# One order for all pieces of an mLSTM and MLP kernel, with output stores on another queue and merged loads

## The chip, the cores and the metric

The kernel runs on one core of a Trainium2 chip. The metric is the device time of one execution in microseconds (us); less is better. The engines named below are PE (matrix products), PEld (its weight loads), DVE (vector), ACT (scalar and activation), POOL, and SP, which here does nothing but issue transfers and wait. Each takes its instructions in program order.

## The reference

A gated linear recurrence (mLSTM) feeds a two-layer MLP. Batch 4, 8 heads, 768 tokens, head size 40; the MLP has 320 inputs, 2048 hidden columns and 320 outputs on 3072 tokens.

```
m_new = max(f[t] + m, i[t]);  fs = exp(f[t] + m - m_new);  is = exp(i[t] - m_new)
C = fs * C + is * outer(v[t], k[t]);   n = fs * n + is * k[t]
y[t] = sigmoid(o[t]) * (C @ q[t]) / max(|n . q[t]|, 1)
h = y @ w_in;   g = h * sigmoid(h);   out = g @ w_out
```

## The kernel before, in words

The recurrence is computed in chunks of 128 tokens. A **unit** n is one chunk of one batch row, all eight heads; there are 24, and chunk c of a row needs the state that chunk c-1 left. `perform` (L871) reads the string `ORDER` (L50 to L102) word by word and emits each word's instructions; the place of a word in the string is its place in the stream of every engine that it uses. The words of a unit, in the order in which one unit needs them:

- `qk`, `kvo`, `d`, `lq` (L445 to L480): loads on SP's queue of q and k (two transfers of 160 KB), of k, v and the output gate, of the decay matrix D (four transfers) and of the decays (four).
- `s` (L493): for units 0 to 3, PE spreads the decays into PSUM instead of `d`; `e` (L513): eight exponentials on ACT; `k` (L522): POOL's causal mask; `r`, `l`, `t`: small ACT pieces; `v` (L538): DVE weights v; `q` (L553): POOL scales q.
- `S` (L615) scores and `P` (L560) products on PE, `w` (L618) and `c` (L576) on DVE, `c` with a POOL multiply between two DVE operations.
- `V` (L622) and `Q` (L640): values and state queries on PE. `V` ends with a `nop` on SP that waits for V's last matmul, and Q's first matmul waits for that nop (the fence, L637). Where a unit's scores go half by half into one bank, L612 puts another such nop on SP. A transfer that stands behind a nop on SP is issued after it.
- `g` (L660) gates and normalizes on DVE in five operations, `x` (L680) transposes on PE, `h` and `y` (L692, L696) split the result into a rounded high part and a rest.

The weights arrive as 64-bit floats and are turned into 32-bit values on the chip, in eight parts each of w_in (`i0` to `i7`, with `c0` and `c4` for its last 64 rows) and w_out (`o0` to `o7`). The words of a part are `L` load (SP), `M` (ACT), `S`, `Z`, `J` (DVE, L318 to L347), and for w_in `T` (ACT, L364) and `R` (DVE, L369). `gs gu gm go gt gf` are the gate scans of one chunk, mostly DVE, `gf` with small matmuls; `go` stores the decays to DRAM.

The MLP of units 0 to 3 is the **opening** (512 tokens): per hidden block of 128 columns `m` (PE, L712), `a` (ACT, L750), `b` (DVE, L755), `n` (PE, L766 to L769), as kinds A (units 0 and 1), B (2 and 3) and J (all four, blocks 4 to 15). The other units come two by two in **steps** 1 to 10. A step has eight slots (`slot`, L906); a slot is 16 matmuls of the first product (L712), tanh and multiply (`glu`, L813), a split into high and low (`halves`, L822) and 12 matmuls of the second product (L841) of two slots earlier. `place` (L930) hangs the pieces of the units onto the slots: at slots 2 and 5 of a step stand P, V, S and Q. When a step's last second product is done, `put` (L721) copies each unit's result on ACT and issues its store on ACT's own queue (L725). `split_out` (L382) rounds w_out in the first eight slots of step 1. `z*8` (`spin`, L862) is eight bf16 matmuls on constants at the start.

In `ORDER`, the blocks of the opening's MLP from block 4 on come in pairs: load and convert the next parts, two `m`, two `n`, one unit's attention. The lines below are four such lines.

```
Lo3 Mi2 Si2 Zi2 Ji2 Ti2 Ri2
Mo2 So2 Zo2 Jo2
mJ4 aJ4 bJ4
mJ5 aJ5 bJ5
```

Of the kernel before, what the change touches and what calls it, by code (L numbers as in the profile page):

```python
# [50 lines left out]
qk0 kvo0 gs0 gu0 gm0 go0 gt0 z*8 s0.0 s0.1 gf0 lq0 Li0 Lc0 qk1 kvo1 Lo0 Mi0 e0.0 e0.1 r0 k0.0 k0.1 v0 S0.0 S0.1 P0 l0 q0 w0 c0  # L51
Si0 Zi0 Ji0 Ti0 Ri0 Mc0 Sc0 Zc0 Jc0 Tc0 Rc0 s1.0 s1.1 lq1 e1.0 e1.1 r1 k1.0 k1.1 v1 P1 V0 S1.0 S1.1 Q0 t0 g0 x0 h0 y0 l1 q1 w1 c1 Li1 qk2 qk3 Mo0 So0 Zo0 Jo0
kvo2 s2.0 s2.1 lq2 e2.0 e2.1 r2 k2.0 k2.1 v2 P2 V1 S2.0 S2.1 Q1 t1 g1 x1 h1 y1 l2 q2 w2 c2 mA0 aA0 bA0 mA1 aA1 bA1 Mi1 Si1 Zi1 Ji1 Ti1 Ri1 Lo1 Li2
nA0 nA1 mA2 aA2 bA2 kvo3 s3.0 s3.1 lq3 e3.0 e3.1 r3 k3.0 k3.1 v3 P3 V2 S3.0 S3.1 Q2 t2 g2 l3 q3 w3 c3 x2 h2 y2 Mo1 So1 Zo1 Jo1 V3 mA3 aA3 bA3 Q3 t3 g3 x3 h3 y3 nA2 nA3 gs1 gu1 gm1 gt1 gf1 go1 gs2 gu2 gm2 gt2 gf2 go2
mB0 aB0 bB0 mB1 aB1 bB1 nB0 nB1 mB2 aB2 bB2 mB3 aB3 bB3 nB2 nB3
Li3
Lo2 Mi2 Si2 Zi2 Ji2 Ti2 Ri2
Mo2 So2 Zo2 Jo2
mJ4 aJ4 bJ4
mJ5 aJ5 bJ5  # L60
qk4 kvo4 d4 lq4 k4.0 k4.1 e4.0 e4.1 v4 l4
Li4 Lc4
Lo3 Mi3 Si3 Zi3 Ji3 Ti3 Ri3
Mo3 So3 Zo3 Jo3
mJ6 aJ6 bJ6
nJ4
mJ7 aJ7 bJ7
nJ5
S4.0 P4 S4.1 w4 q4 c4
Li5  # L70
Lo4 Mi4 Si4 Zi4 Ji4 Ti4 Ri4
Mc4 Sc4 Zc4 Jc4 Tc4 Rc4
Mo4 So4 Zo4 Jo4
mJ8 aJ8 bJ8
nJ6
mJ9 aJ9 bJ9
nJ7
qk5 kvo5 d5 lq5 k5.0 k5.1 e5.0 e5.1 v5 l5
Li6
Lo5 Mi5 Si5 Zi5 Ji5 Ti5 Ri5  # L80
Mo5 So5 Zo5 Jo5
# [24 lines left out]
def mlstm_mlp_kernel(  # L106
# [614 lines left out]
    def put(n, halves, ob):  # L721
        c, b = n // B, n % B
        for cs, po in halves:
            nc.scalar.activation(ob[:, cs], po, AF.Copy, scale=0.5)
        nc.scalar.dma_start(out[b * S + c * L : b * S + (c + 1) * L, :], ob)  # L725

    class Opening:
# [31 lines left out]
        def mm2(self, kind, fc):  # L759
# [3 lines left out]
            for u in sorted(range(u0, u1), key=lambda u: -(u > 2)):  # L763
# [8 lines left out]
                if last and u == 2:  # L772
                    self.store(2)
                if last and u == 1:
                    for k in (0, 1, 3):
                        self.store(k)

        def store(self, u):
# [10 lines left out]
            if u >= 2:
                big.give(f"ob{u}")  # L790

    class Step:
# [19 lines left out]

        def glu(self, s):  # L813
            j, ph = self.j, self.ph.pop(s)
            th = p2.tile([128, FPS * NT], F32, tag="th", name=f"th{j}_{s}")
# [4 lines left out]
            self.g[s] = th  # L820

        def halves(self, s):  # L822
            j, g = self.j, self.g[s]
            t = p3.tile([128, 2, FPS * NT], F32R, tag="g", name=f"g{j}_{s}")
            gh, gl = t[:, 0], t[:, 1]
            nc.scalar.copy(gh, g)  # L826
            nc.vector.tensor_tensor(out=gl, in0=g, in1=gh.bitcast(F32), op=ALU.subtract)  # L827
            self.g[s] = (gh, gl)
# [41 lines left out]

    def perform(order):  # L871

        for word in order.split():
# [1 line left out]
            what, n, hf, times = m[1], m[2] and int(m[2]), m[3] and int(m[3]), int(m[4] or 1)
            u = units[n] if what in UNIT else None
            for _ in range(times):
                if what in UNIT:
                    f = getattr(u, UNIT[what])
                    f() if hf == "" or hf is None else f(hf)  # L880
                elif what in PART:
                    getattr(part[what[-1] + str(n)], PART[what])()
                elif what in GATE:
                    getattr(first, GATE[what])(n, 1)
                elif what in MLP:
# [171 lines left out]
```

## Time and profile before

| what | us |
|---|---|
| median of three runs (lowest to highest) | 578.83 (577.93 to 580.23) |
| the profiled execution: its own time | 580.62 |
| its span, first to last instruction | 578.9 |
| start of the opening's first product (mA0) | 50.68 |
| start of step 1's first product | 197.78 |
| start of step 3's first product | 282.16 |

The profile lists every instruction with its start, its length and what released it. A line such as "PE psum<-xh,wh x8 [4.37 <-ACT wh L364]" reads: eight matmuls, before the first of which PE was idle for 4.37 us until ACT's instruction at L364 was done. PEclk is the share of the full TensorE clock that was granted; 1.0 is 2.4 GHz, 0.5 is 1.2 GHz. Before 54.1 us the trace holds no record of the clock and shows 1.00.

### The profile page before, as it was taken

The numbers are of one execution on the slowest core, as the hardware profiler recorded it, in microseconds if no ns is written. First come the engines' busy times: TensorE is split into PE (matmuls) and PEld (weight loads), VectorE is DVE, ScalarE is ACT, GpSimd is POOL, SyncE is SP. The second block draws the span as 40 slices with busy tenths as digits, with TensorE's granted clock in tenths as the row PEclk, the third lists the DMA queues.
The fourth block names the chain that finished last, engine by engine and source line by source line (L and its number), as shares of the span: only waits on it lengthen the run. The fifth ranks groups of instructions, "written<-read, shape, count | busy, mean of one in ns | idle before, by whom it ended". The sixth has DMA issues, their size and how long they took to land.

```text
span 578.9 us, 13625 instructions
## 1 busy us (share of the span) xinstructions
PE 484.7 (84%) x5760; PEld 444.2 (77%) x5760; DVE 274.6 (47%) x541; ACT 220.0 (38%) x512; POOL 88.4 (15%) x127
## 2 busy tenths in 40 slices
PE   5256678566866888998998989989899899899997
PEld 3245557344744777998998989989899899899997
DVE  1543264545355266655455544554554445444332
ACT  2322212423123065544454335434444345433332
POOL 2321201102011012201222022210221222100000
PEclk9999678687867898999999989999999899999999
DMA  5343008143060352332133221320223203000000
GB/s 164 102 129 128 2 6 245 40 139 112 9 205 2 89 164 68 89 98 77 26 112 87 71 70 59 112 89 26 88 87 108 80 12 110 2 25 1 1 24 23
DMA packets 26269, 44.63 MB, mean 77 GB/s; under 512 B 4384, under 2 KB 16608, under 8 KB 26208
## 3 DMA queue, kind: packets, MB, share of 16 engines
q1 hardware_dynamic: 22688, 39.75, 23.3%
q10 hardware_dynamic: 3520, 4.01, 2.0%
q8 instruction: 45, 0.74, 0.5%
q14 instruction: 16, 0.13, 0.1%
HBM read 39.71 MB, written 4.03 MB: 76 GB/s over the span
## 4 chain that ended last, share of the span: by engine, by line
PE 60%; issue 16%; DVE 11%; ACT 6%; DMA 3%; POOL 2%; SPq 1%; ACTq 0%; DVEq 0%; POOLq 0%
PE psum L712 31%; PE psum L841 16%; DVE th L817 3%; ACT th L816 3%; PE psum L568 2%; DMA D<-LFd 2%; PE psum L601 2%; PE psum L766 2%; DVE D L620 2%; PE psum L649 2%; PE psum L630 2%; PE psum L684 1%; DVE vw L542 1%; ACT D L518 1%; POOL qt L555 1%
## 5 line engine op out<-in xcount | busy, mean ns | idle before, releaser
L841 PE MATMUL psum<-woh,g 128*128 128x320 f32 x640 | 153.9, 310 | 0.0
L712 PE MATMUL psum<-xh,wh 128*128 128x256 f32 x480 | 140.6, 300 | 5.3 <-DVE D L620 4.7
L712 PE MATMUL psum<-xl,wh 128*128 128x256 f32 x480 | 135.2, 289 | 0.0
L841 PEld LDWEIGHTS psum<-woh,g 128*128 128x128 f32 x640 | 110.8, 189 | 0.0
L712 PEld LDWEIGHTS psum<-xh,wh 128*128 128x128 f32 x480 | 94.3, 197 | 11.0 <-DVE D L620 9.2
L816 ACT ACTIVATE th<-psum 128x512 f32<-128x512 f32 x80 | 47.8, 597 | 137.7 <-PE psum L712 125.4
L841 PE MATMUL psum<-wol,g 128*128 128x320 f32 x320 | 99.0, 309 | 0.0
L817 DVE SCALAR_TENSOR_TENSOR th<-th,psum 128x512 f32<-128x512 f32 x80 | 54.9, 686 | 84.7 <-ACT th L816 84.7
L712 PEld LDWEIGHTS psum<-xl,wh 128*128 128x128 f32 x480 | 94.5, 197 | 0.4 <-DVE xl L698 0.3
L712 PE MATMUL psum<-xh,wl 128*128 128x256 f32 x320 | 92.4, 289 | 0.0
L827 DVE TENSOR_TENSOR g<-th,g 128x512 fp32r<-128x512 f32 x80 | 59.0, 738 | 54.9 <-ACT g L826 53.6
L712 PE MATMUL psum<-X,wh 128*128 128x512 f32 (+1 forms) x120 | 44.2, 467 | 32.4 <-ACT wh L364 29.6
L826 ACT CAST g<-th 128x512 fp32r<-128x512 f32 x80 | 49.5, 619 | 53.4 <-DVE th L817 48.4
L712 PEld LDWEIGHTS psum<-xh,wl 128*128 128x128 f32 x320 | 63.1, 197 | 0.0
L841 PEld LDWEIGHTS psum<-wol,g 128*128 128x128 f32 x320 | 60.5, 189 | 0.0
L712 PEld LDWEIGHTS psum<-X,wh 128*128 128x128 f32 x120 | 27.5, 258 | 40.4 <-ACT wh L364 32.6
L524 POOL TENSOR_SCALAR_AFFINE_SELECT D<-D 64x512 f32<-64x512 f32 x48 | 34.8, 724 | 114.3 <-DMA D<-LFd 81.3
L586 POOL TENSOR_TENSOR S<-S,eq 104x164 f32<-104x164 f32 x20 | 9.3, 464 | 246.9 <-DVE S L584 242.8
L568 PE MATMUL psum<-vw,kvo 64*64 64x41 f32 x704 | 17.9, 244 | 33.0 <-DVE vw L542 33.0
L568 PEld LDWEIGHTS psum<-vw,kvo 64*64 64x64 f32 x704 | 14.9, 149 | 38.7 <-DVE vw L542 35.9
L518 ACT ACTIVATE D<-D,aT 128x64 f32<-128x64 f32 x160 | 41.7, 334 | 5.3 <-POOL D L524 5.3
L555 POOL TENSOR_TENSOR qt<-raw,eq 104x512 f32<-104x512 f32 x24 | 30.8, 1285 | 39.4 <-issue 39.2
(114 smaller groups left out, 558.8 us busy)
## 6 DMA issues: line engine op xcount, KB each, us to landing
kvo<-in_kvo_dram SPq DMA_DIRECT2D x24, 484.0 KB
raw<-in_qk_dram SPq DMA_DIRECT2D x48, 160.0 KB
wro<-in_w_out_dram SPq DMA_DIRECT2D x8, 640.0 KB
D<-LFd SPq DMA_DIRECT2D x80, 64.0 KB
wri<-in_w_in_dram SPq DMA_DIRECT2D x8, 512.0 KB
lq<-LFd SPq DMA_DIRECT2D x96, 40.0 KB
out_dram<-ob ACTq DMA_DIRECT2D x24, 160.0 KB
wrc<-in_w_in_dram SPq DMA_DIRECT2D x4, 256.0 KB
```

The lines of the kernel that those rows point to most:

```text
L518: nc.scalar.activation(d[:, j, :], e[:, j, :], AF.Exp, bias=aT[:, self.c, hf, r : r + 1])
L524: nc.gpsimd.affine_select(out=d, in_=d, compare_op=ALU.is_ge, fill=0.0 if self.n < WIDE else NEG, base=0, pattern=[[0, H], [1, LB]], chann ...
L555: nc.gpsimd.tensor_tensor(out=self.qt, in0=self.q[:KP], in1=self.eq, op=ALU.mult)
L568: nc.tensor.matmul(Z[hf * 64 : (hf + 1) * 64, k * HF + j, D1 : 2 * D1], self.kt[rs, h * D : h * D + 64], self.vw[rs, h, :], start=True, st ...
L601: m = nc.tensor.matmul(self.ps[r * 64 : (r + 1) * 64, hf, j, :], self.k[rows, r ^ hf, j, :], self.q[rows, r ^ hf, j, :], start=True, stop= ...
L620: nc.vector.tensor_tensor(out=d, in0=self.ps, in1=d, op=ALU.mult)
L712: nc.tensor.matmul(ph, w, x, start=(i == 0), stop=(i == len(ops) - 1))
L816: nc.scalar.activation(th, ph, AF.Tanh, scale=0.5)
L817: nc.vector.scalar_tensor_tensor(out=th, in0=th, scalar=1.0, in1=ph, op0=ALU.add, op1=ALU.mult)
L826: nc.scalar.copy(gh, g)
L827: nc.vector.tensor_tensor(out=gl, in0=g, in1=gh.bitcast(F32), op=ALU.subtract)
L841: nc.tensor.matmul(self.po[t], g[:, ts], w, start=(fc == 0 and i == 0), stop=(last and i == len(ops) - 1),)
```

## The change

`ORDER` now holds the whole program, the steps included; `slot`, `place` and what calls them are gone, and `tanh`, `glu`, `high` and `low` are words of their own (`a`, `b`, `f`, `F`), as are the two halves of `split_out` (`uh`, `ul`), the copy of a result (`O`) and its store (`D`). `m1.0` is the first product of slot 0 of step 1. From `m3.0` on the words stand in the sequence in which `slot` and `place` emitted them. Up to there the sequence is new. Its words up to `m1.0`:

```
Li1 gs0 Mi1 gu0 gs1 Lc0 gm0 kvo0 Si1 gt0 z7*23 s0.1 gu1 gf0 Zi1 go0 Mc0 s0.0 Sc0 s1.0 qk0 gm1 s1.1 e0.0 Zc0 gt1 Jc0 e0.1
r0 Tc0 Li0 v0 k0.1 Ji1 Rc0 lq0 kvo1 z7*11 S0 k0.0 e1.1 Mi0 l0 lq1 w0 e1.0 P0 Si0 qk1 r1 c0 kvo2 Zi0 s2.1 lq2 t0 qk2 v1
q0 Ti1 e2.1 Ji0 s2.0 z7*12 V0 k1.1 l1 Q0 g0 Lo0 s3.1 e2.0 r2 k1.0 z7*1 S1 Ti0 w1 P1 t2 q1 e3.1 s3.0 c1 t1 e3.0 kvo3 v2
gf1 z7*3 V1 qk3 Ri0 Lo1 r3 go1 Q1 P2 l2 Ri1 k2.1 g1 k2.0 z2*1 x0 S2 c2 lq3 w2 h0 x1 Mo0 z7*3 V2 Li2 Lo2 q2 Q2 S3 h1 y1
So0 y0 k3.0 g2 k3.1 t3 v3 Zo0 mA0 mA2 aA0 bA0 l3 P3 mA1 w3 lq4 c3 x2 Mo1 Li4 So1 V3 aA2 qk4 bA2 Jo0 aA1 q3 mA3 d4 h2 Zo1
Mi2 y2 Li3 d5 nA0 aA3 Jo1 Q3 Mo2 g3 Mi4 nA2 x3 bA3 Si2 Lc4 bA1 h3 l4 Zi2 y3 nA3 Ji2 Ti2 So2 k4.1 nA1 mB0 Li5 kvo4 Ri2
Zo2 mJ4 aB0 aJ4 kvo5 bB0 mB2 nB0 aB2 gs2 bJ4 k5.1 Si4 Mc4 bB2 Jo2 Mi3 Zi4 Lo3 Si3 Ji4 k5.0 Sc4 k4.0 mJ5 Zc4 e4.1 e4.0
aJ5 Ti4 nB2 v4 mB1 Zi3 Li6 bJ5 q4 Jc4 aB1 bB1 Ji3 e5.0 nJ4 nJ5 S4.0 Lo4 Ti3 lq5 P4 Tc4 Ri4 qk5 Lo5 Ri3 t5 S4.1 Mi6 Li7
c4 gu2 mJ6 aJ6 Rc4 e5.1 nB1 mJ7 Mo3 bJ6 Mo4 gm2 w4 mJ9 V4 v5 S5.0 So3 Zo3 Si6 So4 Q4 qk6 gt2 Jo3 t4 Mi5 Lo7 l5 aJ7 go2
Lo6 S5.1 Si5 aJ9 P5 Zi5 bJ7 bJ9 nJ6 d6 lq6 g4 mJ8 Zo4 mB3 Ji5 k6.0 Jo4 w5 Zi6 k6.1 aB3 Ji6 d7 aJ8 bJ8 Mo5 nJ7 Ti5 Ri5
So5 x4 lq7 h4 nJ9 Zo5 Mo7 bB3 mJ10 Ti6 Jo5 aJ10 c5 y4 mJ11 kvo6 q5 lq8 gf2 e6.0 bJ10 Ri6 gl Mi7 V5 S6.0 Si7 So7 Q5 e6.1
k7.0 aJ11 Zi7 Ji7 S6.1 v6 mJ12 w6 kvo8 gs3 nJ10 nB3 qk7 Mo6 g5 Ti7 Zo7 nJ8 Ri7 k7.1 l6 d8 bJ11 So6 x5 mJ15 aJ12 h5 t6
bJ12 Zo6 nJ11 kvo7 mJ13 P6 q6 l8 Jo6 V6 aJ15 bJ15 d9 e7.0 aJ13 k8.0 mJ14 c6 l7 nJ12 k8.1 uh0 uh1 bJ13 aJ14 Q6 qk8 y5
bJ14 m1.0
```

`z7*23` is 23 spins into PSUM bank 7. The rest of the change:

```diff
@@ load_raw: q and k
-                    t[hf * 64 : hf * 64 + D].rearrange("p w k j t -> p (w k j t)"), qk[n, hf]
+                    t[hf * 64 : hf * 64 + D].rearrange("p w k j t -> p w (k j t)"),
+                    qk[n, hf].rearrange("p (w f) -> p w f", w=2),
@@ load_d: two transfers in place of four (load_lq: the same)
+            hs, ks = NC * 2 * NB * LB, NB * LB
             for r in range(2):
-                for hf in range(2):
...
+                at = LFd[0, c, r, b * HF : (b + 1) * HF]
+                nc.sync.dma_start(
+                    self.Dm[r * 64 : (r + 1) * 64].rearrange("p (f j) t -> p f (j t)", f=2),
+                    bass.AP(at.tensor, at.offset, [[0, 64], [hs + (1 - 2 * r) * ks, 2], [1, HF * LB]]),
+                )
@@ products: P's first matmul waits for the last Q before it
+                        if first and Unit.fenced:
+                            after(m, Unit.fenced)
+                        first = False
@@ queries
+            Unit.fenced = nc.sync.nop()
+            after(Unit.fenced, m)
@@ put becomes copy (ACT) and sent (SP)
-        for cs, po in halves:
-            nc.scalar.activation(ob[:, cs], po, AF.Copy, scale=0.5)
-        nc.scalar.dma_start(out[b * S + c * L : b * S + (c + 1) * L, :], ob)
+        nc.sync.dma_start(out[b * S + c * L : b * S + (c + 1) * L, :], obs.pop(n))
```

## Rows read from the trace of the kernel before

**Rows 1.** The page: the span, and busy time by engine.
```profile
span 578.9 us, 13625 instructions
PE 484.7 (84%) x5760; PEld 444.2 (77%) x5760; DVE 274.6 (47%) x541; ACT 220.0 (38%) x512; POOL 88.4 (15%) x127
PE   5256678566866888998998989989899899899997
```

**Rows 2.** Busy time by stretch: opening, steps 1 and 2, step 3, the rest.
```profile
core 0: us, PE busy (x) PEld busy (x) DVE busy (x) ACT busy (x) POOL busy (x), PEclk, DMA share, GB/s
0.00:197.80 197.80, 126.54 (x1253) 98.18 (x1253) 86.55 (x169) 52.34 (x130) 28.78 (x45) 0.83 0.33 97
197.80:282.10 84.30, 77.71 (x986) 73.35 (x987) 48.26 (x98) 42.21 (x102) 18.30 (x26) 0.94 0.34 97
282.10:319.20 37.10, 35.05 (x488) 33.95 (x487) 18.82 (x38) 16.97 (x41) 7.25 (x10) 1.00 0.26 78
282.10:578.90 296.80, 280.42 (x3524) 272.67 (x3522) 139.82 (x275) 125.41 (x281) 41.37 (x56) 0.99 0.19 58
```

**Rows 3.** Waits, 0 to 198 us: total us, times, longest; SP's own last.
```profile
PE psum L712 <- ACT wh L364: 29.6, 7, 7.0
PE psum L568 <- DVE vw L542: 21.3, 4, 8.6
PE psum L684 <- DVE x L674: 8.2, 5, 1.7
...
SPq L612 <- PE psum L601: 70.9, 3, 24.4
SPq L637 <- PE psum L630: 49.6, 6, 19.0
```

**Rows 4.** Timeline of one opening pair, 122.2 to 126.9 us: start, length, instruction.
```profile
122.23 0.37 SPq L297 DMA_DIRECT2D wri<-in_w_in_dram  x1
...
124.27 0.42 DVE L320 TENSOR_SCALAR wti<-wti 128x512 uint32<-128x512 uint32 x1
...
126.18 0.62 ACT L364 CAST wh<-wti 128x512 fp32r<-128x512 f32 x1 [6.15 <-DVE wti L340]
...
126.85 1.22 PE L712 MATMUL psum<-X,wh 128*128 128x512 f32 x2 [4.37 <-ACT wh L364]
```

**Rows 5.** Busy time in a stretch at 0.5 and one at 1.0 of the clock.
```profile
125.80:136.00 10.20, 8.20 (x19) 5.67 (x19) 7.19 (x11) 3.83 (x6) 1.94 (x2) 0.50 0.87 253
115.60:125.70 10.10, 6.88 (x87) 5.24 (x86) 3.21 (x7) 1.16 (x2) 0.46 (x1) 1.00 0.22 69
```

**Rows 6.** DVE's timeline: its first scan, and a hand-over to POOL and back.
```profile
3.32 0.42 DVE L197 TENSOR_TENSOR_SCAN G<-G 48x128 f32<-48x128 f32 x1 [2.38 <-DMA G<-in_ig_dram]
...
49.85 0.68 DVE L620 TENSOR_TENSOR D<-psum,D 128x512 f32<-128x512 f32 x1
...
51.74 0.32 DVE L587 TENSOR_TENSOR S<-S,psum 104x164 f32<-104x164 f32 x1 [0.98 <-POOL S L586]
```

**Rows 7.** PE's timeline: one matmul of 512 columns at either clock, and the eight spins.
```profile
1.00 3.60 PE L864 MATMUL psum<-G 128*128 128x512 bf16 x8 [1.00 <-DVE G L898]
...
117.28 0.40 PE L712 MATMUL psum<-X,wl 128*128 128x512 f32 x1
...
127.87 0.63 PE L712 MATMUL psum<-X,wl 128*128 128x512 f32 x1
```

**Rows 8.** Timeline of step 3's end: result copies, their stores, and the next attention.
```profile
402.07 0.44 ACT L724 ACTIVATE ob<-psum 128x320 f32<-128x320 f32 x1 [0.66 <-PE psum L841]
...
402.90 0.66 PE L630 MATMUL psum<-kvo,D 64*64 64x41 f32 x32
402.93 0.44 ACT L724 ACTIVATE ob<-psum 128x320 f32<-128x320 f32 x1 [0.41 <-ACT ob L724]
...
403.39 0.34 ACTq L725 DMA_DIRECT2D out_dram<-ob  x1
```

**Rows 9.** The page: packets of SP's queue and its share of the 16 DMA engines.
```profile
q1 hardware_dynamic: 22688, 39.75, 23.3%
```

More of the change, by code (lines that the diff above doesn't have):

```diff
@@ L50 @@
 ORDER = """
[L51 to L81, printed above, removed]
@@ L391, in split_out, with split_low @@
             wol[i] = wraw.take("wol0", [128, 2, DM], F32R)
-        nc.scalar.copy(hi, full)
-        nc.vector.tensor_tensor(out=wol[i], in0=full, in1=hi.bitcast(F32), op=ALU.subtract)
+        nc.scalar.copy(rounded(slice(2 * i, 2 * i + 2)), wo[i])
+    def split_low(i):
+        hi = rounded(slice(2 * i, 2 * i + 2))
+        nc.vector.tensor_tensor(
+            out=wol[i], in0=wo.pop(i), in1=hi.bitcast(F32), op=ALU.subtract
+        )
     parts = []
@@ L430, in mlstm_mlp_kernel @@
     class Unit:
+        fenced = None
         def __init__(self, n):
@@ L562, in products @@
             self.pu = [Z[:KP, k * HF : (k + 1) * HF, D1 : 2 * D1] for k in range(2)]
+            first = True
             for j in range(HF):
@@ L771, in mm2, with copy @@
                     )
[L772 to L778, printed above, removed]
+        def copy(self, u):
             if u < 2:
@@ L819, in glu, with high, low @@
             )
[L820 to L828, printed above, removed]
+        def high(self, s):
+            t = p3.tile([128, 2, FPS * NT], F32R, tag="g", name=f"g{self.j}_{s}")
+            self.g[s] = t[:, 0], t[:, 1]
+            nc.scalar.copy(t[:, 0], self.th[s])
+        def low(self, s):
+            gh, gl = self.g[s]
+            nc.vector.tensor_tensor(
+                out=gl, in0=self.th.pop(s), in1=gh.bitcast(F32), op=ALU.subtract
+            )
         def mm2(self, s):
@@ L869, in mlstm_mlp_kernel, with gate_word @@
     opening = steps[0] = Opening()
+    late = []
+    def gate_word(what, n):
+        if what == "gl":
+            late.append(gates_late())
+        elif n < 3:
+            getattr(first, GATE[what])(n, 1)
+        else:
+            getattr(late[0], GATE[what])(3, NC - 3)
+            if what == "gf":
+                big.give("lfi", "lml")
     def perform(order):
@@ L874, in perform @@
             m = re.fullmatch(r"([a-zA-Z]+)(\d*)(?:\.(\d))?(?:\*(\d+))?", word)
[L875 to L885, printed above, removed]
-                    getattr(opening, MLP[what])(what[-1], n)
-                else:
-                    spin(1)
+            what, n, k, times = m[1], int(m[2] or 0), m[3] and int(m[3]), int(m[4] or 1)
+            if what in UNIT:
+                getattr(units[n], UNIT[what])(*([] if k is None else [k]))
+            elif what in STEP:
+                getattr(steps[n], STEP[what])(k)
+            elif what in PART:
+                getattr(part[what[-1] + str(n)], PART[what])()
+            elif what in OTHER:
+                OTHER[what](n)
+            elif what in MLP:
+                getattr(opening, MLP[what])(what[-1], n)
+            elif what == "z":
+                spin(times, n)
+            else:
+                gate_word(what, n)
+    STEP = dict(m="mm1", a="tanh", b="glu", f="high", F="low", n="mm2")
     UNIT = dict(qk="load_raw", kvo="load_kvo", d="load_d", lq="load_lq", s="spread", e="exps",
@@ L897, in mlstm_mlp_kernel @@
     MLP = {a + b: f for a, f in dict(m="mm1", a="tanh", b="glu", n="mm2").items() for b in "ABJ"}
+    OTHER = dict(uh=split_high, ul=split_low, O=copied, D=sent)
     nc.vector.memset(busy, 1.0)
     perform(ORDER)
-    def run(*calls):
-        for f in calls:
-            f()
-    def slot(j, s, first=(), early=(), middle=(), end=()):
-        st = steps[j]
-        run(*first)
-        st.mm1(s)
-        run(*early)
-        st.glu(s)
-        run(*middle)
-        if s >= LAG:
-            st.mm2(s - LAG)
-        elif j > 1:
-            steps[j - 1].mm2(NSL - LAG + s)
-        else:
-            opening.mm2("J", NFC - LAG + s)
-        st.halves(s)
-        run(*end)
@@ L962, in mlstm_mlp_kernel @@
-    for n in range(DONE, NU):
-        place(n)
-    late = gates_late()
-    rest = (3, NC - 3)
-    at(0, "end", lambda: late.scan(*rest))
-    at(1, "middle", lambda: late.sub(*rest))
-    at(2, "middle", lambda: late.sum(*rest))
-    at(2, "end", lambda: late.store(*rest))
-    at(3, "middle", lambda: late.top(*rest))
-    at(4, "first", lambda: late.flip(*rest), lambda: big.give("lfi", "lml"))
-    for i in range(DFF // 256):
-        at(i, "middle", lambda i=i: split_out(i))
-    for j in range(1, NSTEP):
-        for s in range(NSL):
-            slot(j, s, **pieces.get((j - 1) * NSL + s, {}))
@@ L978, in mlstm_mlp_kernel @@
-    for s in range(NSL - LAG, NSL):
-        steps[NSTEP - 1].mm2(s)
 def _layout(inputs):
```

155 lines of the change are left out of this document (71 added, 84 removed).

## The prediction

> **What bounds the kernel now.** I read the page first [rows 1]: PE is busy for 484.7 of 578.9 us, far more than DVE or ACT, so PE is the engine to follow, and 94 us of the span are without it. The question is where these lie. The sums by stretch [rows 2] answer it: step 3 takes 37.10 us with PE busy for 35.05, and from the start of step 3 to the end it is 280.42 of 296.80. There only 16 us are to be had, and the change leaves the sequence of those words as it was. The opening is another matter: 197.80 us, with PE busy for 126.54, DVE for 86.55, ACT for 52.34, and DMA at a share of 0.33. No engine is full. Steps 1 and 2 are nearly full (77.71 of 84.30).
>
> The waits of the opening [rows 3] say what PE stood for: 29.6 us in seven waits for a rounded weight part (`T`, L364), 21.3 us in four for `v`, 8.2 us for `g`'s result. SP, which issues all loads, stood for 120.5 us in its two kinds of nop. One pair shows how these hang together [rows 4]: SP issues the next weight part only after a score fence, DVE begins the three conversions of the part before it at 124.27, ACT rounds at 126.18 after 6.15 us of idling, and PE starts 4.37 us late. Load, convert, multiply and attend stand one after another in the string, and each engine takes them in that order. So the opening is bounded by hand-overs, not by work.
>
> The clock follows from this. In a stretch in which PE was busy for 8.20 of 10.20 us after such a wait the granted share was 0.50, the lower level of 1.2 GHz; in another, busy for 6.88 of 10.10 after dense products, it was 1.00, the 2.4 GHz level [rows 5]. A 512-column matmul takes 0.63 us at the one and 0.40 at the other, the pipeline's tail included [rows 7].
>
> **The parts and their costs.** (a) The opening up to `m1.0`. The words are the same; the new string only puts them side by side, so the time cannot fall below the fullest engine's work. For DVE that is the 86.55 us of before [rows 2] plus what now precedes `m1.0`: `w6` 0.68, `c6` 0.65 (two of 0.32) [rows 6] and the scan `gs3` (384 columns, by the 128-column scan's 0.42 about 1.1 with its copy), together 89 us. For PE it is 126.54 plus 46 more spins, which cost 0.45 us each at the lower clock (eight in 3.60 [rows 7]) and by the ratio of the two levels half of it at the upper, so 10 to 21 us, plus the moved `V6` and `Q6` of 0.66 us each [rows 8]. That is 138 to 149 us if the clock stays as it was. If it is mostly up, the products shrink towards 0.40 for 0.63: 126.54 x 0.63 is 80, and with spins and attention 92 us. So DVE and PE come out nearly equal, and what they wait for each other decides.
>
> DVE's waits in the new sequence, in order. It starts at 3.32 us, when the gates land [rows 6]. It then works some 3.5 us and stops at `gf0`, whose matmuls stand behind 23 spins: these end between 8 and 11 us (all low after the first eight, or all high), so about 3 us. Seven `c`, each with a POOL multiply between two DVE operations that stand next to each other, wait 0.98 us each [rows 6]: 7 us. About ten places remain where a part waits for ACT or for a raw buffer that a `J` has just freed (`Jo3` then `Mi5` then `Si5` is one), at about 1 us: 10 us. I add 7 us for `b` and `g` behind PE where the clock is down. Sum 30, so `m1.0` starts at 89 + 30 = 119 us. The bounds are 104 (half of the waits) and 150 (the clock as before, next part). The gain is 197.8 - 119 = 79 us.
>
> (b) `m1.0` to `m3.0`. PE's words are the same but for `nJ13` more and `V6`, `Q6` fewer, which cancel at some 1.3 us. PE was busy for 77.71 us at a mean clock of 0.94 [rows 2]; 10 us at half clock cost it 5 of these, so 72.7 at the upper level. With step 3's idling (2.05 in 37.10) it comes to 77 us, bounds 73 and 84.3: a gain of 7.
>
> (c) From `m3.0` on: 296.8 as before [rows 2]. Two things are new there. The stores move from ACT to SP: ACT no longer loses the 0.41 us behind each [rows 8], but its waits end on DVE and PE there, so I count nothing. On SP the two stores of a step stand ahead of the next unit's V fence. ACT finishes the second copy at 403.37 in the old sequence and about 0.4 us earlier without its own store; SP then issues a store (0.34), by 403.4, and V ends at 403.56 [rows 8]. It just fits. If it does not, Q comes up to 0.4 us late in each of eight steps, 3 us: bounds 0 and 3. The nop behind every Q delays the q and k loads that follow on SP by Q's length, under 1 us; they are for three units later. In the opening P waits for that nop: P2 stands directly behind Q1, whose nop is behind three issues on SP, so some 1.5 us, which is among the ten places of (a).
>
> (d) Loads. Merging four D and four decay transfers into two each halves their issues on SP, which is hidden, since SP waited for 120 us anyway [rows 3]. About 20 MB land before `m1.0` (97 GB/s for 197.8 us [rows 2]); at the 253 GB/s that a share of 0.87 gave [rows 5] the engines would carry 290, so 69 us of 119: hidden, though no longer far off. The 2 KB packets add 80 a unit. SP's queue took 23.3% of 16 engines for 22688 packets [rows 9], 95 ns each; nine units bring 720 more, 4.3 us of all engines if each costs a full one, nothing if bytes alone count. I take nothing, since half of the engines' time is free. The Trainium skill's page "DMA: Bandwidth & Descriptors", section "Rules for kernel authors", speaks against this part: many small transfers should be made into one large one; by it the 4.3 us would be paid, and the forecast would be 497. No run here shows packets of either size side by side.
>
> Sum: 119 + 77 + 296.8 = 492.8 us of span, against 578.9. Around the span lie 580.62 - 578.9 = 1.7 us, so 494.5 for the profiled execution; that one stood 1.8 us above the median of 578.83. Predicted: **493 us**.
>
> **The rivals.** *The clock stays down.* Up to `mA0` the new string mixes short attention matmuls with waits, and the clock may fall there and after each wait, as it did before [rows 5]. PE then needs its 138 to 149 us, and is the bound: `m1.0` at 150, and with 80 for (b) the result is 150 + 80 + 296.8 - 0.1 = 527. For it: 0.50 was granted even at 80% busy. Against: most stops that PE made before, 59 us [rows 3], are what the new sequence fills, and spins stand ahead of `S0`, `V0`, `V1` and `V2`. The Trainium skill's page "TensorE: Matmul & The Clock Gate", section "Loop structure matters more than you think", states that bursts of matmuls between long waits run cold; rows 4 and 5 agree (a 4.37 us wait, then 0.50).
>
> *The hand-overs nearly vanish.* DVE runs with half of my waits, `m1.0` at 104, (b) at 73: 104 + 73 + 296.8 - 0.1 = 474. For it: ACT works only 52 us, and there are always two or three units and two parts in flight. Against: three raw buffers for units, three for parts, two PSUM banks for the products.
>
> *The old serial order half returns.* With buffers as few as before, loads behind the 17 nops before `m1.0` come late at a few places, and half of the 79 us comes back: 532. *Slower than before.* The same nops on SP decide: the longest waits were 24.4 and 19.0 us [rows 3]. If four times a weight part that DVE needs next is queued behind a V or Q that itself waits that long, 4 x 22 = 88 us come on top of 493, and the kernel is at 581; from there every further one makes it slower. From `o0` on the load of a part stands 22 to 87 words ahead of its `M`, which speaks against it. *No effect:* the waits were not what bounds the opening, and it stays near 579.
>
> **How the numbers follow.** My forecast (478 to 508) has 0.5, the quick case 0.15, the clock 0.2, the half return 0.1, slower 0.03 and no effect 0.02. The range takes in the quick case and the clock's and reaches into the half return: 468 to 530; above and below stay about 0.2. A measurement of this kernel tells about 0.5% from no change. Faster by more than that: 0.95; within: 0.02; slower: 0.03.
>
> **What the new profile would show.** Right: PE's L712 with X starts before 42 us; `m1.0`, the first L712 with xh, near 119; DVE busy for about 75% up to it; SP's waits at L637 no longer followed by a PE wait for L364; 297 us from the start of step 3. Wrong: a granted clock of 0.50 over half of 40 to 119 us (the clock); PE waiting for `T` or `v` by more than 20 us in the opening (the serial order); DMA share over 0.8 for tens of us; a remainder over 300 us (the stores on SP).

## The result: 494.1 us, and the profile after

Median 494.11 us of four runs (490.88 to 495.18), against 579.48 (577.93 to 580.23) for four runs of the kernel before beside it: ratio 0.852, 95% interval 0.848 to 0.857. The profiled execution took 493.72 us. The first products of each stage in the two profiled executions:

| first product of | before, us | after, us | gained up to there |
|---|---|---|---|
| block 0 of the opening (mA0) | 50.68 | 44.25 | 6.4 |
| block 4, the first J (mJ4) | 99.00 | 60.34 | 38.7 |
| step 1 (m1.0) | 197.78 | 121.94 | 75.8 |
| step 3 (m3.0) | 282.16 | 196.78 | 85.4 |
| end of the span | 578.9 | 492.0 | 86.9 |

(At mJ4 the two have not done the same work: after, three of the four B blocks and the gate scan of chunk 2 still lie behind it.) The page after, against [rows 1]; PEclk is the granted clock in tenths, in 40 equal slices of the span:

```profile
span 492.0 us, 13627 instructions
PE 463.2 (94%) x5802; PEld 423.7 (86%) x5806; DVE 270.9 (55%) x541; ACT 217.9 (44%) x512; POOL 93.9 (19%) x127
PEclk9857999989999999999999999999998999999999
```

PE's share went from 84% to 94%. Its busy time fell by 21.5 us too, though it has 42 matmul records more: the same products run at the upper level of the clock. The rest, 65 us, is idle time that is gone. Busy time by stretch, which answers to [rows 2] (its columns):

```profile
0.00:44.20 44.20, 35.75 (x568) 22.20 (x572) 24.60 (x55) 18.11 (x54) 16.61 (x29) 0.77 0.52 161
44.20:121.90 77.70, 75.14 (x785) 59.87 (x780) 58.37 (x118) 37.58 (x85) 18.64 (x22) 0.98 0.59 181
0.00:121.90 121.90, 110.88 (x1348) 82.07 (x1352) 82.97 (x172) 55.69 (x139) 35.25 (x51) 0.90 0.56 174
121.90:196.70 74.80, 73.21 (x940) 70.34 (x933) 47.87 (x94) 37.67 (x94) 13.90 (x18) 1.00 0.29 83
196.70:492.00 295.30, 279.16 (x3524) 271.34 (x3522) 140.08 (x275) 124.58 (x281) 44.76 (x59) 0.99 0.21 58
```

From mA0 to m1.0 PE hardly stands: it is busy for 75.14 of 77.70 us. What idling is left in the opening lies mostly ahead of mA0, 8.45 of 44.2 us, with a granted clock of 0.77 (the record of the clock begins at 5.0 us here; before that the view shows 1.00). The waits of PE from 44 to 122 us, against [rows 3], where the conversions alone (L364) stood for 29.6 us:

```profile
PE psum L725 <- DVE g0A L776: 0.9, 1, 0.9
PE psum L697 <- DVE D L631: 0.9, 1, 0.9
PE psum L241 <- DVE xl L711: 0.4, 1, 0.4
PE psum L697 <- DVE x L687: 0.3, 1, 0.3
```

No wait for a weight part or for a weighted `v` is left in the whole opening. SP still waits, though less than the 120.5 us of [rows 3]: its nops, 0 to 122 us (total, times, longest):

```profile
SPq L648 <- PE psum L641: 47.4, 7, 11.8
SPq L623 <- PE psum L612: 13.9, 3, 13.1
```

None of PE's waits is for a transfer that is queued behind them, and DVE's only wait for a transfer is that for the gates, ahead of its first scan. POOL does wait, 28.0 us in four waits for D, beside 35.25 us of work. What PE still pays at the nops themselves is 1.15 us before P2 (e9 below) and 0.6 us before three `Q`.

### The profile page after: what moved, and what is told of

It reads as the page before. It is cut to its first block, busy times and chain, and to the rows that moved or that the text cites. A ratio compares the mean times of both kernels' runs of the same rounds, so it can differ in the third digit from the quotient of the medians.

```text
span 492.0 us, 13627 instructions
## 1 busy us (share of the span) xinstructions
PE 463.2 (94%) x5802; PEld 423.7 (86%) x5806; DVE 270.9 (55%) x541; ACT 217.9 (44%) x512; POOL 93.9 (19%) x127
## 3 DMA queue, kind: packets, MB, share of 16 engines
q1 hardware_dynamic: 25024, 43.68, 30.2%
## 4 chain that ended last, share of the span: by engine, by line
PE 72%; DVE 9%; DMA 6%; issue 5%; ACT 4%; POOL 2%; SPq 2%; ACTq 0%; POOLq 0%; DVEq 0%
PE psum L725 35%; PE psum L863 21%; DVE th L837 3%; DVE D L631 2%; ACT th L833 2%; PE psum L787 2%; PE psum L576 2%; PE psum L641 2%; DMA D<-LFd 2%; PE psum L612 2%; PE psum L660 2%; PE psum L883 1%; PE psum L697 1%; DMA wrc<-in_w_in_dram 1%; DMA raw<-in_qk_dram 1%
## 5 line engine op out<-in xcount | busy, mean ns | idle before, releaser
L725 PE MATMUL psum<-xh,wh 128*128 128x256 f32 x480 | 137.4, 294 | 5.5 <-DVE D L631 5.5
L725 PE MATMUL psum<-xl,wh 128*128 128x256 f32 x480 | 132.7, 284 | 0.0
L837 DVE SCALAR_TENSOR_TENSOR th<-th,psum 128x512 f32<-128x512 f32 x80 | 54.9, 686 | 85.4 <-ACT th L833 85.4
L725 PEld LDWEIGHTS psum<-xh,wh 128*128 128x128 f32 x480 | 92.2, 192 | 10.1 <-DVE D L631 9.3
L725 PEld LDWEIGHTS psum<-xl,wh 128*128 128x128 f32 x480 | 92.4, 192 | 0.1
L725 PE MATMUL psum<-xh,wl 128*128 128x256 f32 x320 | 90.9, 284 | 0.0
L725 PEld LDWEIGHTS psum<-xh,wl 128*128 128x128 f32 x320 | 61.6, 192 | 0.0
L531 POOL TENSOR_SCALAR_AFFINE_SELECT D<-D 64x512 f32<-64x512 f32 x48 | 38.0, 792 | 88.1 <-DMA D<-LFd 59.3
L725 PE MATMUL psum<-X,wh 128*128 128x512 f32 (+1 forms) x120 | 33.8, 378 | 0.9 <-DVE g0A L776 0.9
L562 POOL TENSOR_TENSOR qt<-raw,eq 104x512 f32<-104x512 f32 x24 | 31.8, 1326 | 9.9 <-PE psum L725 5.8
L576 PE MATMUL psum<-vw,kvo 64*64 64x41 f32 x704 | 17.0, 236 | 10.2 <-DVE vw L549 9.0
L576 PEld LDWEIGHTS psum<-vw,kvo 64*64 64x64 f32 x704 | 14.3, 142 | 14.3 <-DVE vw L549 10.5
L725 PEld LDWEIGHTS psum<-X,wh 128*128 128x128 f32 x120 | 21.3, 194 | 5.1 <-DVE g0A L776 1.0
```

The lines of the kernel that those rows point to most:

```text
L531: nc.gpsimd.affine_select(out=d, in_=d, compare_op=ALU.is_ge, fill=0.0 if self.n < WIDE else NEG, base=0, pattern=[[0, H], [1, LB]], chann ...
L562: nc.gpsimd.tensor_tensor(out=self.qt, in0=self.q[:KP], in1=self.eq, op=ALU.mult)
L576: m = nc.tensor.matmul(Z[hf * 64 : (hf + 1) * 64, k * HF + j, D1 : 2 * D1], self.kt[rs, h * D : h * D + 64], self.vw[rs, h, :], start=True ...
L725: nc.tensor.matmul(ph, w, x, start=(i == 0), stop=(i == len(ops) - 1))
L837: nc.vector.scalar_tensor_tensor(out=th, in0=th, scalar=1.0, in1=ph, op0=ALU.add, op1=ALU.mult)
```

## Experiments

Two theories stood against each other at first. **Mine:** the gain is the order of words; the loads and the queue of the stores count for nothing; what now sets the opening is PE's and DVE's own work. **The rival:** a part of the gain comes from the merged transfers or from the stores' move, and PE is still waiting, not working. Each median below stands beside runs of the kernel before on the same chip; ratios are to those.

**e1: the change with the old loads** (q and k in 4 KB rows, four transfers of D and four of decays a unit).

```diff
-   qk[n, hf].rearrange("p (w f) -> p w f", w=2)
+   qk[n, hf]
-   for r in range(2): one dma_start of D          (load_lq: the same)
+   for r in range(2): for hf in range(2): one dma_start of D
```

> The changed kernel with the loads of before: D and decays by four transfers a unit each, q and k in 4 KB packets. If the order alone makes the gain (my theory): 494 us within 3, m1.0 at 122 within 2. If the merged loads carry part of it (rival): SP issues 16 more transfers for units 4 to 8 at 0.3 to 0.6 us each and about as many decay loads, 10 us of issue time before m1.0, so m1.0 later by 5 us or more and about 500 us. If the 2 KB packets cost what each extra packet takes (the page's rule), going back gains up to 4 us: 490.

Measured: 493.29 us (490.96 to 494.05), ratio 0.852 [0.848, 0.857]; m1.0 at 122.83, m3.0 at 197.95, within 1.2 us of the change's. **e7: the kernel before with the new loads alone.**

> The kernel before with the new loads alone: D and decays by two transfers, q and k in 2 KB packets. Theory: SP waits for its nops for 120 us of the opening, so its issue time is hidden: 579 us within 3. Rival: D lands earlier, and POOL's 39 us of waiting for D shorten: 574 or less.

Measured: 580.68 us, ratio 1.002 [0.999, 1.006], over ten runs. So the loads do nothing that these intervals show, in either order. The pages say what became of the packets; total packets, bytes, and SP's queue with its share of 16 engines, first of the change, then of e1:

```profile
DMA packets 25148, 44.62 MB, mean 91 GB/s; under 512 B 3264, under 2 KB 15488, under 8 KB 25088
q1 hardware_dynamic: 25024, 43.68, 30.2%
```

```profile
DMA packets 26270, 44.64 MB, mean 91 GB/s; under 512 B 4384, under 2 KB 16608, under 8 KB 26208
q1 hardware_dynamic: 26144, 43.69, 30.2%
```

The new loads have 1120 packets fewer on SP's queue, and 1120 fewer under 512 B; between 512 B and 8 KB the counts are equal, so the rows of q and k came as the same packets either way. The engines' share stays at 30.2%: neither the small packets saved nor the shorter rows of q and k are to be seen in it.

**e2: the change with the stores back on ACT's queue.**

```diff
-   nc.sync.dma_start(out[...], obs.pop(n))
+   nc.scalar.dma_start(out[...], obs.pop(n))
```

> The changed kernel with the 24 result stores issued by ACT again, at the same place in the order. Theory: nothing hangs on them, the time from m3.0 to the end stays at 295 us within 1 and the whole at 494 within 3. Rival: ACT's 0.8 us for two stores and the wait behind each is on the path at the start of each step, 8 steps by 0.8 us, so about 500.

Measured: 495.36 us (493.68 to 496.95), ratio 0.857 [0.852, 0.861]: no difference that its interval tells from the change's. From m3.0 to the end it took 296.8 us against 295.2, but its steps hold two stretches at the lower clock and the change's one; without any, e3 and e5 took 293.8 us for the same part. So each such stretch costs about 1.5 us, and the stores' queue costs nothing that these runs show, on either engine.

**e3 and e4: more work on one engine.** e3 makes PE do the first product twice for six of the J blocks; the result is that of the second time. e4 makes DVE run the last conversion of every w_out part and the split of every full w_in part twice.

```diff
e3, Opening.mm1
+   for _ in range(2 if kind == "J" and fc in (5, 6, 8, 10, 12, 13) else 1):
        first_product(ph, fc, xh0, xl0, slice(u0 * L, u1 * L))
e4, Part.lows (w_out) and Part.rest
+   for _ in range(2 if self.i is not None else 1): nc.vector.scalar_tensor_tensor(...)
+   for full, hi, lo in self.halves() * (2 if self.K == 128 else 1):
```

> The changed kernel with the first product of six J blocks (5, 6, 8, 10, 12, 13) computed twice into the same bank: 48 more matmuls of 512 columns, 6 x 1.9 = 11 us more PE work at the upper clock and nothing else. If PE is the bound from 44 us on, as its 75.14 of 77.70 us say: m1.0 later by 11 us, about 505 us in all. If DVE and its waits are the bound, as my sum had it (89 us of DVE work and 30 of waits): PE has room and m1.0 moves by less than 4 us.

> The changed kernel with sixteen DVE conversions done twice (the subtraction of each of the eight w_in parts, 0.69 us, and the last conversion of each of the eight w_out parts, 0.83 us): 12 us more DVE work before m1.0, and nothing else. If PE is the bound from 44 us on: less than 4 us later, since DVE is busy for 58 of 78 us there. If DVE is the bound, as in my sum: m1.0 later by 10 to 12 us, about 505 us.

Measured: e3 502.71 us (502.30 to 507.24), ratio 0.871 [0.866, 0.877]; e4 502.69 us (501.10 to 503.83), ratio 0.869 [0.863, 0.874]. m1.0 came at 132.26 and 131.36, that is 10.3 and 9.4 us late. The stretch from mA0 to m1.0 (columns as in [rows 2]), e3, then e4:

```profile
43.50:132.20 88.70, 86.57 (x830) 69.71 (x828) 60.31 (x116) 37.50 (x85) 18.83 (x22) 0.97 0.50 158
```

```profile
44.00:131.30 87.30, 79.80 (x783) 61.32 (x780) 70.71 (x130) 37.61 (x85) 17.93 (x22) 0.94 0.51 161
```

In e3 PE has 11.4 us more to do and the stretch is 11.0 us longer: PE is the bound there, all of its work counts. But e4 falls on the other side of what I had expected. DVE has 12.3 us more to do, had stood idle for 19 of 77.70 us, and still the stretch grew by 9.6. Half of that is PE standing (7.5 us idle in place of 2.6), at places such as these three of PE's timeline:

```profile
64.58 0.73 PE L726 MATMUL psum<-X,wh 128*128 128x512 f32 x2 [1.12 <-ACT wh L363]
...
66.03 0.50 PE L726 MATMUL psum<-X,wl 128*128 128x512 f32 x1 [0.72 <-DVE wl L368]
...
119.46 0.70 PE L726 MATMUL psum<-X,wh 128*128 128x512 f32 x2 [1.24 <-DVE g0J L777]
```

The other half is PE being busy for 4.7 us longer with two matmul records fewer, at a granted clock of 0.94 in place of 0.98. So DVE's results reach PE just in time: at these places DVE's idle time is no reserve, and the stretch has two bounds at once. Two things stay open. Both doubled operations stand directly ahead of a hand-over to PE, and whether 12 us put elsewhere on DVE would cost as much was not tried. And not all of the 12.3 us are the doubling: one conversion, at 61.19 us, took 2.69 us beside a POOL multiply (see the last section).

**e5 and e6: the spins.** e5 takes out every `z` word of the change, e6 every one but the first (`z7*23`).

```diff
- ... gm0 kvo0 Si1 gt0 z7*23 s0.1 ... kvo1 z7*11 S0 ... s2.0 z7*12 V0 ... gf1 z7*3 V1 ...
+ ... gm0 kvo0 Si1 gt0 s0.1 ... kvo1 S0 ... s2.0 V0 ... gf1 V1 ...          (e5)
```

> The changed kernel without any spin; the rest of the order as it is. If the spins hold the clock for the first 44 us: the attention of units 0 to 3 and the first products run at the lower clock, mA0 later by 5 us or more, about 500 us. If they stand in the chain (my reading of the profile: the clock is down from 18.7 to 22.1 and from 25.5 to 42.6 us all the same, gf0 waits behind 23 of them and V0 behind 11, 4.45 us): mA0 earlier by 2 to 6 us, 489 to 493.

> The changed kernel with the first 23 spins only; the 31 later ones are left out. If the later ones hold the clock: mA0 later than 44.25 us by 3 or more. If they stand in the chain: V0 starts at 17 to 18 us in place of 22.30, but DVE's conversions stand ahead of g0 until 22.4, so mA0 is earlier by 1 to 4 us only, 490 to 493 in all.

Measured: e5 489.02 us (486.68 to 492.37), ratio 0.844 [0.839, 0.850]; e6 489.11 us (487.05 to 491.55), ratio 0.844 [0.840, 0.849]. mA0 starts at 39.13 and 40.51 in place of 44.25, m1.0 at 119.92 and 118.19 in place of 121.94. The medians are 5 us lower, but both intervals overlap the change's at their edges (0.848 to 0.857), and a part may be no doing of the spins: behind m3.0 the profiled execution of the change has one stretch at the lower clock (370.3 to 373.7 us), worth 1.5 us by e2, where theirs have none. So the later spins cost some 2 to 4 us up to m1.0, and the first 23 change nothing that can be measured. In the change's own trace the later ones stand in the way. PE's timeline:

```profile
1.00 7.16 PE L883 MATMUL psum<-G 128*128 128x512 bf16 x23 [1.00 <-DVE G L932]
...
17.92 4.45 PE L883 MATMUL psum<-G 128*128 128x512 bf16 x11 [2.96 <-DVE S L598]
22.30 0.68 PE L641 MATMUL psum<-kvo,D 64*64 64x41 f32 x32
```

The 12 spins ahead of `V0` first wait 2.96 us for unit 0's `c` (L598) and then hold PE for 4.45 us; `V0` follows at once. (The wait itself is not theirs: in e5 `V0` waits for the same instruction, until 16.58 us.) And the spins raise the clock for a time only. The record shows 1.00 from 5.0 to 18.7 and from 22.1 to 25.5 us in the change, and from 7.0 to 13.8 us in e6, but then the change ran at the lower level until mA0 was near.

```profile
25.50:42.60 17.10, 13.70 (x230) 9.59 (x227) 7.47 (x18) 4.94 (x15) 4.87 (x7) 0.50 0.39 134
```

e6 had the lower level from 13.8 to 44.5 us. e5's record begins only at 44.2 us, at 1.00, but 32 matmuls of `V1` took 1.09 us in it at 25.15, as at the lower level. Both reach mA0 earlier all the same: PE's work ahead of it is short attention matmuls behind hand-overs, and 32 of them at 1.09 us in place of 0.66 [rows 8] cost less than the spins do. e5 loses 3.1 of its 5.1 us again up to m1.0 (80.80 us from mA0, against 77.68), with its first products at the lower level.

**e9: e5, and P2 no longer next to the nop of Q1.** In both e5 and the change DVE's longest wait of the first 44 us is that of unit 1's `g` (L677), released by unit 2's `P` (L576), which stands between Q1 and `g1` in the string and itself waits for the nop behind Q1. Lines of three timelines of the change, SP's, PE's and DVE's:

```profile
31.70 0.68 SPq L454 DMA_DIRECT2D raw<-in_qk_dram  x2
32.41 0.40 SPq L295 DMA_DIRECT2D wro<-in_w_out_dram  x1
32.85 0.93 SPq L257 DMA_DIRECT2D LFd<-G  x2
...
33.94 1.09 PE L576 MATMUL psum<-vw,kvo 64*64 64x41 f32 x32 [1.15 <-issue]
...
35.09 0.17 DVE L677 TENSOR_SCALAR nq<-psum 128x8 f32<-128x8 f32 x1 [4.53 <-PE psum L576]
```

SP is issuing the transfers of three words (`qk3`, `Lo1`, `go1`) until 33.78; only then the nop can pass, and P2 starts at 33.94. (The trace names no releaser for P2; that it waits for the nop is in the code, and the times fit.) `g1` begins as P2 ends (33.94 + 1.09 = 35.03), 2.3 us after Q1, which ends at 32.79. e9 puts `g1` and what follows it before these issues and P2 later:

```diff
- gf1 V1 qk3 Ri0 Lo1 r3 go1 Q1 P2 l2 Ri1 k2.1 g1 k2.0 x0 S2 c2 lq3 w2 h0 x1 Mo0
+ gf1 V1 Ri0 r3 Q1 x0 g1 h0 qk3 Lo1 go1 l2 Ri1 k2.1 P2 k2.0 S2 c2 lq3 w2 x1 Mo0
```

> The changed kernel without spins and with seven words moved around unit 1's gate: g1 now stands ahead of P2 (in e5 it waited 3.95 us for P2, which itself waited 2.01 us for the nop behind three issues on SP), those three issues (qk3, Lo1, go1) stand behind Q1's nop, and x0 and h0 stand ahead of unit 2's scores. If that wait is on the chain of the first 40 us: mA0 at 36 to 37.5 us in place of 39.13 and the whole at 486 to 488. If DVE's and PE's work behind it is what counts: m1.0 stays at 119 to 120 and the whole at 489.

Measured: 486.25 us (484.14 to 490.28, six runs), ratio 0.840 [0.836, 0.844]. The interval lies below the change's, so this one beats both kernels. `g1`'s wait, at the same place in DVE's sequence, and P2 in PE's, in e9:

```profile
28.84 0.17 DVE L629 TENSOR_SCALAR nq<-psum 128x8 f32<-128x8 f32 x1 [1.43 <-PE psum L612]
...
30.19 1.09 PE L528 MATMUL psum<-vw,kvo 64*64 64x41 f32 x32
```

It is 1.43 us in place of 3.95 in e5 and 4.53 in the change, and it ends with unit 1's own queries (L612 there), so `g1` had no need of P2; why its release came with P2 the traces don't show (in the code P2 and Q1 write into the same two PSUM banks, `Z`). P2 itself starts without a wait, where it had waited 2.01 us in e5. mA0 starts at 37.96, just behind the 36 to 37.5 us of the one theory, and m1.0 at 118.50, just ahead of the 119 to 120 of the other. The intervals of e9 and e5 (486.25 and 489.02 us) overlap, so what the move of `g1` alone is worth stays open. That P could start without the wait for Q's nop was not tried: the wait keeps the two apart, and taking it away alone would be a race.

**e8 and e10: the order in parts, from the side of the kernel before.** A second question was which hand-over the gain came from. e8 is the kernel before with the loads and conversions of parts `i3` to `i7` and `o3` to `o7` moved half a pair ahead, nothing else; e10 also loads each unit a pair earlier and puts the attention of units 4 to 6 between the products of a pair.

```diff
e8
- Lo3 Mi3 Si3 Zi3 Ji3 Ti3 Ri3 Mo3 So3 Zo3 Jo3 mJ6 aJ6 bJ6 nJ4 mJ7 aJ7 bJ7 nJ5
+ mJ4 aJ4 bJ4 Mi3 Si3 Zi3 Ji3 mJ5 aJ5 bJ5 Ti3 Ri3 ... Mo3 So3 Zo3 Jo3
+ mJ6 aJ6 bJ6 Li5 Lo4 Mi4 Si4 Zi4 Ji4 nJ4 mJ7 aJ7 bJ7 Ti4 Ri4 ... nJ5
e10, on top of it
- S4.0 P4 S4.1 w4 q4 c4
+ mJ6 aJ6 bJ6 Li5 Lo4 Mi4 Si4 Zi4 Ji4 P4 S4.0 nJ4 S4.1 w4 q4 mJ7 aJ7 bJ7 Ti4 Ri4 c4 ...
```

> The kernel before with the loads and conversions of the weight parts from i3 on moved half a pair ahead in its string (between the two products of the pair before); attention, products and steps stay where they were. If the hand-over of the weight parts is what PE waits for (29.6 us in seven waits for T): five or six of these waits shrink from 4 to 7 us to under 1, 20 to 30 us less, 550 to 560 us. If the wait only moves on (DVE is late with b, or the clock stays down because attention still stands alone): less than 10 us less, 570 or more.

> The kernel before with the conversions moved as in e8 and, besides, the loads of units 4 to 8 one pair earlier and the attention of units 4 to 6 inside the pairs, between an n and an m; everything up to block 3 and from step 1 on as before. If standing apart costs the attention as it did the conversions: the 5 to 7 us that each of the three attention stretches and their D loads keep PE waiting mostly go, 15 to 25 us less than e8's 547, 522 to 532. If the conversions were the only hand-over that counted: 540 or more. What then remains to the changed kernel lies in the first 98 us and in steps 1 and 2.

Measured: e8 547.17 us (541.90 to 548.76), ratio 0.943 [0.936, 0.949]; e10 542.73 us (541.61 to 547.97), ratio 0.939 [0.933, 0.945]. e8 alone gains 31 us on the 578.21 of its own runs of before, a little more than I had expected and over a third of the change's 85. (The profiled executions of the two, which the rows below are from, are the quickest of their four each, 541.90 and 541.61 us.) PE's timeline of e8 shows the first products of the pairs that in the kernel before stood behind 4 to 7 us for `T` [rows 3, 4]; two of them, the first ended by the `R` of a c part (L339), the second by `T` (L334):

```profile
118.66 0.73 PE L682 MATMUL psum<-X,wh 128*128 128x512 f32 x2 [1.36 <-DVE wh L339]
...
126.40 0.73 PE L682 MATMUL psum<-X,wh 128*128 128x512 f32 x2 [0.82 <-ACT wh L334]
```

From 98 us on PE's waits for `T` sum to 4.5 us in place of 28.3, the longest 2.4, and mJ4 to m1.0 takes 63.7 us (99.1 to 162.81) in place of 98.8. The change takes 61.6 (60.34 to 121.94), with three B blocks more in it. So most of what the old opening lost behind mJ4 is this one hand-over. The clock went with it: the same stretch, before and in e8:

```profile
99.00:163.00 64.00, 42.90 (x321) 32.06 (x321) 32.13 (x51) 19.20 (x42) 6.40 (x8) 0.76 0.32 98
```

```profile
99.00:163.00 64.00, 54.97 (x527) 41.34 (x527) 46.43 (x77) 28.00 (x63) 12.12 (x14) 1.00 0.45 132
```

e10 added nothing that its interval can tell from e8, which is the outcome that I had named for "the conversions only". But it does not decide that question. Its timeline shows why it got no further: the attention words between the products moved the conversions behind them, and PE again waited for them, with a lower clock from 121.6 to 131.8 us. Its m1.0 comes 3.3 us later than e8's (166.08), its steps 1 and 2 take 3.5 us less (79.98 in place of 83.50).

```profile
105.83 0.73 PE L682 MATMUL psum<-X,wh 128*128 128x512 f32 x2 [2.81 <-ACT wh L334]
...
121.34 1.04 PE L682 MATMUL psum<-X,wh 128*128 128x512 f32 x2 [3.26 <-DVE wh L339]
```

In e8 as in e10 mJ4 still starts at 99 us. The 38.7 us that the change gains up to there, by running units 0 to 3, the A and B blocks and the parts beside each other, were not taken apart by a run, nor were the 9.5 us of steps 1 and 2 (84.38 to 74.85).

## Why the prediction was right, and where it was off

**The sum.** Predicted 119 us to m1.0, 77 to m3.0, 296.8 to the end; measured 121.9, 74.8 and 295.2. The errors, +2.9, -2.2 and -1.6, nearly cancel, so the 493 is better than its terms.

**(a), what sets the opening: mis-sized on PE.** The step gave PE 92 us if the clock is mostly up, and let DVE with its waits set the time. PE was busy for 110.88 us. Of the 19 us more, some 5 are spins: the 50 of them that the trace recorded took 17.0 us, where the 92 held 10 for the new ones and 3.6 x 0.63 = 2.3 for the old. Some 5.5 are half of the other work, 11.0 us, in the 20.5 us at the lower level ahead of mA0 (18.7 to 22.1 and 25.5 to 42.6). The rest, some 9 us, is the factor: 126.54 x 0.63 shrank all of the old work, but much of it had run at 1.00 already. The old trace's stretches at 1.00 up to m1.0, those at 0.50, and the part ahead of its clock record:

```profile
sum 75.00, PE 50.99 PEld 37.62 DVE 30.03 ACT 18.74 POOL 5.63; mean PE 5.67 PEld 4.18 DVE 3.34 ACT 2.08 POOL 0.63
sum 68.70, PE 48.90 PEld 39.14 DVE 36.73 ACT 19.21 POOL 9.17; mean PE 5.43 PEld 4.35 DVE 4.08 ACT 2.13 POOL 1.02
0.00:54.10 54.10, 26.66 (x424) 21.42 (x425) 19.79 (x45) 14.39 (x42) 13.98 (x27) 1.00 0.45 140
```

With only the 48.90 halved, and the 26.66 too (`P1` took 1.09 us at 27.66 there, as at the lower level), the old work comes to 89 us and not 80. From mA0 on PE is full, and e3 shows that it is the bound, where my sum had left it room; e4 shows that DVE is one too, which the step had said ("nearly equal, and what they wait for each other decides"). That the sum for DVE still gave 119 is in part luck: its work and its waits were both off, the one up and the other down.

**(a), DVE's work and waits.** Work 82.97 us for my 89, waits 39 for my 30. Three sizes: `gf0` behind the 23 spins waited 2.31 us where I had 3; the hand-over of `c` to POOL and back took 0.58 to 0.68 where I had 0.98; and P2 behind Q1's nop, "some 1.5 us", took 1.15 on PE. But the step stopped at P2 and did not name who stands behind it: `g1` on DVE, which waited 4.53 us there, 2.3 of them after its own queries had ended (e9). `gf0`'s row in DVE's timeline:

```profile
9.36 0.19 DVE L252 TENSOR_SCALAR aT<-psum 128x32 f32<-128x32 f32 x1 [2.31 <-PE psum L246]
```

**(b)** gave 72.7 us of PE's work at the upper level; PE was busy for 73.21 at 1.00. It idled for 1.6 us where I had put 4.3, by step 3's; that is the error.

**(c)** held: 295.2 us, and e2 shows no price of either queue.

**(d)** was right in its result and wrong in its reason. I counted 80 packets more for each unit's q and k, and 720 before m1.0. The count fell instead, by 1120 over the whole program, and the class that fell is that under 512 B. The 95 ns for a packet, from [rows 9], was therefore never put to the test. The Trainium skill's page "DMA: Bandwidth & Descriptors", section "Rules for kernel authors", would have small transfers merged for their overhead. That row speaks of transfers, of which the change has fewer; that it covers packets too was my reading, and the 497 rests on it. Here the D and decay transfers were halved in number and the time did not move (1.002 for the kernel before, 493.29 against 494.11 for the change), with SP waiting in its nops for 61 us anyway. Whether the overhead of a transfer itself went down, no run shows. "Half of the engines' time is free" was right as a mean (0.56 up to m1.0) and wrong in pieces; four stretches of the change (columns as above):

```profile
5.00:15.00 10.00, 9.80 (x191) 6.31 (x190) 7.07 (x17) 5.76 (x18) 3.12 (x2) 1.00 0.93 267
45.00:50.00 5.00, 4.15 (x59) 3.39 (x58) 2.88 (x7) 2.28 (x6) 0.62 (x2) 1.00 0.99 369
55.00:65.00 10.00, 9.69 (x51) 7.46 (x50) 8.44 (x19) 4.34 (x9) 5.37 (x6) 1.00 1.04 303
80.00:95.00 15.00, 15.00 (x190) 12.10 (x189) 13.23 (x26) 6.03 (x11) 1.24 (x2) 1.00 0.83 243
```

For some 40 us the DMA engines are at a share of 0.83 to 1.04 (a transfer counts where it starts, so a stretch can pass 1), and carry up to 369 GB/s, above the 290 that I had worked out from [rows 5]. PE's waits show none for a transfer in these stretches; in the last it never stood.

**The rivals.** *The clock stays down* was right for 21 of the first 44 us and wrong for the rest: 0.98 from mA0 to m1.0, with PE's waits at 2.5 us. *The hand-overs nearly vanish* came true on PE from mA0 on, but not on DVE, whose waits were 39 us and not 15, and not as 474 us, since PE's work itself filled the time. *The old serial order half returns* and *slower* needed PE to wait for parts behind nops on SP; SP waited 61 us in them and no such wait of PE followed.

**Signs named ahead.** mA0 before 42 us: no, 44.25 (e5 and e9, without spins, have it at 39.13 and 37.96). m1.0 near 119: 121.94. DVE busy for 75% up to it: 68%. No PE wait for the rounded part: right. DMA share over 0.8 for tens of us was to be a sign against the prediction; it came and meant nothing for the time, since no wait of PE hung on it.

## What to carry to other kernels

Where engines take their instructions in order and hand over to each other, read who is idle ahead of the full engine's waits and move the preparing words half a stage ahead; one such move (e8) gave a third and more of what the new order of all words gave. Once the full engine no longer waits, test the others' idle time by adding work to them before counting it as reserve: here 12 us on an engine that idled for 19, put directly ahead of hand-overs, cost 9.6. And look at the filler again after a reorder: spins meant to keep the clock up kept it up for a part of the time only and cost more than they gave, some 2 to 4 us. A wait on one engine is to be followed to the engine behind it.

## What was not expected of the hardware

**A DVE operation beside POOL.** The same conversion at L338 took 0.68 us at 12.78 and 2.37 us at 20.07. DVE's timeline, then POOL's:

```profile
12.78 0.68 DVE L338 SCALAR_TENSOR_TENSOR wti<-wri,wti 128x512 uint32<-128x512 uint32 x1
...
17.78 1.50 DVE L325 SCALAR_TENSOR_TENSOR wti<-wri,wti 128x512 uint32<-128x512 uint32 x1
...
20.07 2.37 DVE L338 SCALAR_TENSOR_TENSOR wti<-wri,wti 128x512 uint32<-128x512 uint32 x1
```

```profile
11.82 3.22 POOL L531 TENSOR_SCALAR_AFFINE_SELECT D<-D 64x512 f32<-64x512 f32 x2 [7.11 <-ACT last L543]
...
17.47 1.27 POOL L562 TENSOR_TENSOR qt<-raw,eq 104x512 f32<-104x512 f32 x1
18.81 1.86 POOL L531 TENSOR_SCALAR_AFFINE_SELECT D<-D 64x512 f32<-64x512 f32 x2
20.64 1.25 POOL L562 TENSOR_TENSOR qt<-raw,eq 104x512 f32<-104x512 f32 x1
...
27.90 1.52 POOL L531 TENSOR_SCALAR_AFFINE_SELECT D<-D 64x512 f32<-64x512 f32 x2
```

Each long one ended 0.54 to 0.55 us after a POOL multiply (18.74 and 19.28; 21.89 and 22.44), as if it had run only then. The Trainium skill's page "SBUF — State Buffer", section "Who interferes with whom", states that a DVE instruction with two SBUF inputs contends with a GpSimd instruction that reads SBUF, because its second input comes through a read interface that the two share. These rows agree. The operation at 12.78 ran at full speed beside POOL's masks (L531), but there it was POOL that took longer: 3.22 us for two masks, against 1.52 at 27.90. The other traces show the same pattern: in all twelve kernels the 183 such conversions with no POOL operation beside them took 0.66 to 0.70 us, the 17 beside a multiply for `q` took 1.50 to 2.69, and the 40 beside other POOL work took 0.68 to 1.03. No run took POOL's work away, so the cause is likely and not shown. A conversion is in any case not a constant in an order that puts it beside POOL: 2.5 us more for two operations.

**The clock beside much work.** From 25.5 to 42.6 us PE was busy for 13.70 of 17.10 us at a granted clock of 0.50, the 1.2 GHz level, although three runs of spins, 7.16, 2.35 and 4.45 us, had gone before. The Trainium skill's page "TensorE: Matmul & The Clock Gate", section "Loop structure matters more than you think", tells of matmuls that run cold after long waits; in this stretch PE's longest wait was 1.30 us, so here short waits went with the lower level too.
